# First eight attention units of a fused kernel: diagonal by a second product, natural k through TensorE, and an order written by hand

## The chip, the cores and the metric

The kernel runs on one core of one Trainium2 chip. The metric is the time of the program on the device in microseconds (us), as the median of several runs. Profiles come from one execution each, recorded by the hardware profiler. Engines are named as in the profile: PE (TensorE), with PEld for its weight loads, DVE (VectorE), ACT (ScalarE), POOL (GpSimd) and SP (SyncE, which here only issues transfers).

## The reference

A linear attention with a decaying state (4 batches, 8 heads, 768 tokens, 48 per head) feeds two feed-forward layers (d_model 384, d_ff 2048, 3072 tokens):

```python
for t in range(S):
    kt, vt, rt = (k[:, :, t], v[:, :, t], r[:, :, t])
    cur = np.einsum('bhd,bhe->bhde', u[None] * kt, vt)
    y[:, :, t] = np.einsum('bhd,bhde->bhe', rt, state + cur)
    state = w[None, :, :, None] * state + np.einsum('bhd,bhe->bhde', kt, vt)
...
h = x @ w_in;  g = np.maximum(0.01 * h, h);  x = g @ w_out     # first layer
h = x @ w_in;  g = h * np.cos(h);            out = g @ w_out   # second layer
```

All is float32.

## The kernel before

**Attention.** The 24 units of work are 128 tokens each, two sub-chunks of 64; six units make one batch, and the state goes from unit to unit. A unit loads k transposed (kst, 112x512), r transposed (into ar or rf_), r and k in natural layout (natt, 384 KB) and v. `prep` (L279 to L292) scales kst by inverse powers of the decay (pt[:, 1]) and r by powers (pt[:, 0]), takes the bonus of the diagonal from natt (times ub, times k, summed per head: bon) and scales natural k by the table kn. `piece_a` (L303 to L334) makes 16 score products pa and 16 state products pu, fills ar with a diagonal matrix of bon by eight ACT activations (L321), lays the scores over it under a mask (copy_predicated, L322), and brings the state forward on DVE (L329 to L333). `piece_y1` makes py, copies it to yo on ACT (L371) and writes it to the memory tensor xt by two transfers on POOL's queue (L374). The first eight units (u < ONE) use this form, with tiles lent from weight buffers that are not yet filled.

**Round trip.** `load_xu` (L436 to L441) reads a unit back from xt into xl, on POOL's queue too. Since its first index is a register (the slow path of the kernel writes another half), the read covers all of xt for the dependence tracker: the write of a unit waits until the read of the unit before has landed. `split_xu` casts to xh on ACT (L445) and takes the residual xl on DVE (L446).

**Feed-forward.** Tokens go in six blocks of 512, d_ff in 16 steps of 128. Every float32 product is three products of reduced precision (xl with wh, xh with wl, xh with wh): ph (L458) for the first matrix, po (L498 to L500) for the second. The weights of a step, w0 to w15, are loaded raw in two copies, wr and wo (768 KB each, two buffers of both, L248 and L251), and decoded by `split_w`: sign of wr on ACT (L266), a mask on DVE (L267), relu into wo on ACT (L269), the product for wh on DVE (L270), three more steps on DVE (L271, L273, L275). A buffer is loaded again when its decode is done.

**Order.** The first entries are a list, `first` (prep, attention, output, load and decode of given units), and only ACT follows it word for word (`manual_schedule`); the other engines' order is the scheduler's, which also places instructions of later steps in between. After the list come three more pieces, then blocks 0 and 1 interleaved: (0,0) to (0,7), (0,8), (1,0), (0,9), (1,1) and so on, with the other pieces of units 5 to 7 due between steps. SP issues loads in program order. One head branch (`tc.If(slow > 0)`, L189) separates what stands before it from what stands behind.

Of the kernel before, what the change touches and what calls it, by code (L numbers as in the profile page):

```python
# [58 lines left out]
def moe_rwkv_kernel(ctx: ExitStack, tc, wT, wq, uu, rs, ks, nat, wmoe, out):  # L59
# [114 lines left out]
    kn = ap_.tile([128, H, D], F32, name="kn")
    ps = psum.tile([128, H, D], F32, tag="a0", name="ps_t")
    for i in range(H):
        for c in range(2):
            nc.tensor.matmul(
                out=ps[TOK[c], i], lhsT=(pw[HALF[0], i] if c else pt[HALF[1], 1, i]),
                rhs=ident[ROWS[c], ROWS[c]], start=True, stop=True)  # L180
    nc.scalar.copy(out=kn, in_=ps)
# [96 lines left out]

    def prep(u):  # L279
        t, x, ar = U["nat", u], U["ks", u], ar_[u % 2]  # L280
        bon = ap_.tile([128, H], F32, tag="bon", bufs=2, name="bon")
# [1 line left out]
        if u < ONE:
            nc.vector.tensor_tensor(out=rf_[u % 4], in0=rf_[u % 4], in1=pt[:, 0], op=ALU.mult)
        else:
            for c in range(2):
                nc.vector.tensor_tensor(out=ar[ROWS[c], c], in0=ar[ROWS[c], c], in1=pt[ROWS[c], 0], op=ALU.mult)
# [353 lines left out]
```

## Time and profile before

| what | us |
|---|---|
| median of 3 runs (959.82 to 960.3) | 959.87 |
| span of the profiled execution | 954.9 |
| first MoE product (block 0) | 78.41 |
| first MoE product of block 1 | 137.57 |

Busy in the span: PE 896.4 us (94%), DVE 647.5 (68%), ACT 521.7 (55%), POOL 53.1 (6%). The busy tenths of PE in 40 slices are 1, 6, 4, 8 and then 9 nearly to the end. A busy PE need not be at its peak; the granted clock and the duration of equal products tell its level. A row of the timeline gives start, duration, engine, line, operation, output<-inputs, shapes and count, and in brackets how long the engine had been idle and what released it.

### The profile page before, as it was taken

Reading aid. Unit: us, or ns where it says so; the run is one execution under the profiler, and the core shown is the slowest. Engines: PE = TensorE matmul, PEld = TensorE weight load, DVE = VectorE, ACT = ScalarE, POOL = GpSimd, SP = SyncE. Lnnn points to the kernel's source line nnn. Section 1 sums busy time; section 2 is a strip of 40 time slices with the busy share of each in tenths; the row PEclk is TensorE's granted clock in tenths of the full one; section 3 lists DMA queues with packets and bytes.
Section 4 is the critical chain, followed back from the end, with each engine's and each line's share of the span. In section 5 each row is a group of like instructions: output and inputs, shape, how many; then the busy total and the mean of one; then the engine's idle time right before and its main releaser. Section 6 shows DMA issues by size and latency. Waiting matters only on the chain.

```text
span 954.9 us, 15397 instructions
## 1 busy us (share of the span) xinstructions
PE 896.4 (94%) x5954; PEld 734.8 (77%) x5954; DVE 647.5 (68%) x1072; ACT 521.7 (55%) x1050; POOL 53.1 (6%) x92
## 2 busy tenths in 40 slices
PE   1648979999999999999999999999999999999997
PEld 1646858887778888878888788888888888888886
DVE  7768979449865776675848877565665755665654
ACT  1435545635654564563645566665665655665654
POOL 3111100000100000001000000000000000000000
PEclk9957989999999999999999999999999999999999
DMA  7579786024512322252828910100100100100000
GB/s 191 160 248 310 257 287 187 1 68 131 174 47 65 114 98 89 95 204 74 306 69 276 314 72 1 33 34 1 34 34 1 62 4 9 59 1 0 34 1 34
DMA packets 41277, 99.79 MB, mean 104 GB/s; under 512 B 4976, under 2 KB 8176, under 8 KB 41200
## 3 DMA queue, kind: packets, MB, share of 16 engines
q1 hardware_dynamic: 31552, 75.96, 24.6%
q0 software_dynamic: 4896, 14.16, 4.7%
q10 hardware_dynamic: 4752, 8.65, 2.4%
q8 instruction: 47, 0.77, 0.3%
q14 instruction: 30, 0.25, 0.1%
HBM read 84.59 MB, written 14.16 MB: 103 GB/s over the span
## 4 chain that ended last, share of the span: by engine, by line
PE 75%; DMA 10%; DVE 8%; ACT 3%; issue 2%; SPq 0%; POOL 0%; POOLq 0%; ACTq 0%; DVEq 0%
PE ph L458 35%; PE po L498 12%; PE po L499 12%; PE po L500 12%; DMA wr<-in_wmoe 2%; DMA xl<-xt 2%; PE pa L309 2%; PE py L346 2%; ACT ar L321 1%; DMA natt<-in_nat 1%; DMA xt<-yo 1%; PE pu L316 1%; DVE wh L270 1%; DVE wl L275 1%; DMA wo<-in_wmoe 1%
## 5 line engine op out<-in xcount | busy, mean ns | idle before, releaser
L498 PE MATMUL po<-gh,wl 128*128 128x512 f32 x576 | 228.0, 396 | 2.9 <-ACT gh L485 2.7
L499 PE MATMUL po<-gh,wh 128*128 128x512 f32 x576 | 224.6, 390 | 0.0
L500 PE MATMUL po<-gl,wh 128*128 128x512 f32 x576 | 207.0, 391 | 0.7 <-DVE gl L486 0.7
L486 DVE TENSOR_TENSOR gl<-ga,gh 128x512 fp32r<-128x512 f32 x192 | 132.2, 689 | 94.7 <-ACT gh L485 80.6
L485 ACT CAST gh<-ga 128x512 fp32r<-128x512 f32 x192 | 118.6, 619 | 120.1 <-PE po L499 73.3
L458 PE MATMUL ph<-xl,wh 128*128 128x512 f32 x576 | 169.1, 396 | 5.9 <-DVE xl L446 4.8
L458 PE MATMUL ph<-xh,wh 128*128 128x512 f32 x576 | 168.1, 391 | 0.0
L458 PE MATMUL ph<-xh,wl 128*128 128x512 f32 x576 | 165.0, 392 | 0.0
L458 PEld LDWEIGHTS ph<-xl,wh 128*128 128x128 f32 x576 | 108.2, 190 | 30.7 <-DVE xl L446 5.2
L498 PEld LDWEIGHTS po<-gh,wl 128*128 128x128 f32 x576 | 108.1, 188 | 28.0 <-ACT gh L485 4.1
L458 PEld LDWEIGHTS ph<-xh,wl 128*128 128x128 f32 x576 | 109.0, 189 | 23.1
L500 PEld LDWEIGHTS po<-gl,wh 128*128 128x128 f32 x576 | 107.9, 188 | 24.4 <-DVE gl L486 1.8
L458 PEld LDWEIGHTS ph<-xh,wh 128*128 128x128 f32 x576 | 109.0, 189 | 23.0
L499 PEld LDWEIGHTS po<-gh,wh 128*128 128x128 f32 x576 | 108.2, 188 | 21.4
L321 ACT ACTIVATE ar<-ident,bon 64x64 f32<-64x64 f32 (+1 forms) x320 | 80.7, 333 | 26.6 <-DVE bon L290 26.3
L473 DVE SCALAR_TENSOR_TENSOR gt<-gt,ga 128x512 f32<-128x512 f32 x96 | 65.8, 689 | 38.9 <-ACT gt L472 38.4
L468 DVE TENSOR_TENSOR ga<-ph,ga 128x512 f32<-128x512 f32 x96 | 66.0, 688 | 37.8 <-ACT ga L467 37.4
L478 DVE TENSOR_TENSOR ga<-ph,gt 128x512 f32<-128x512 f32 x96 | 65.8, 689 | 36.3 <-ACT gt L477 35.7
L467 ACT ACTIVATE ga<-ph 128x512 f32<-128x512 f32 x96 | 57.1, 594 | 59.2 <-PE ph L458 56.1
L477 ACT ACTIVATE gt<-gt 128x512 f32<-128x512 f32 x96 | 59.8, 627 | 49.8 <-DVE gt L475 49.7
L471 ACT ACTIVATE ga<-ph 128x512 f32<-128x512 f32 x96 | 57.4, 598 | 44.3 <-PE ph L458 30.3
L472 ACT ACTIVATE gt<-ga 128x512 f32<-128x512 f32 x96 | 60.2, 631 | 1.6
(128 smaller groups left out, 754.0 us busy)
## 6 DMA issues: line engine op xcount, KB each, us to landing
wr<-in_wmoe SPq DMA_DIRECT2D x32, 768.0 KB, 6.0
wo<-in_wmoe SPq DMA_DIRECT2D x32, 767.5 KB, 5.7
natt<-in_nat SPq DMA_DIRECT2D x20, 384.0 KB, 4.1
xt<-yo POOLq DMA_DIRECT2D x48, 96.0 KB, 3.6
x2t<-ob ACTq DMA_DIRECT2D x18, 256.0 KB, 2.0
xl<-x2t POOLq DMA_DIRECT2D x6, 768.0 KB, 4.7
kst<-in_ks SPq DMA_DIRECT2D x20, 224.0 KB, 3.4
vs<-in_nat SPq DMA_DIRECT2D x40, 96.0 KB, 4.1
```

The lines of the kernel that those rows point to most:

```text
L321: nc.scalar.activation(out=ar[q, c, g], in_=ident2[q], func=AF.Copy, scale=bon[q, g:g + 1])
L458: nc.tensor.matmul(out=p, lhsT=w_[:, 0, k * 128:(k + 1) * 128], rhs=x_[:, k], start=(m == 0), stop=(m == 3 * KT - 1))
L468: nc.vector.tensor_tensor(out=ga, in0=p, in1=ga, op=ALU.max)
L472: nc.scalar.activation(out=gt, in_=ga, func=AF.Copy, bias=MAGIC)
L473: nc.vector.scalar_tensor_tensor(out=gt, in0=gt, scalar=MAGIC, in1=ga, op0=ALU.subtract, op1=ALU.subtract)
L477: nc.scalar.activation(out=gt, in_=gt, func=AF.Sin, scale=-TWOPI)
L478: nc.vector.tensor_tensor(out=ga, in0=p, in1=gt, op=ALU.mult)
L485: nc.scalar.copy(out=gh, in_=ga)
L486: nc.vector.tensor_tensor(out=gl, in0=ga, in1=gh.bitcast(F32), op=ALU.subtract)
L498: nc.tensor.matmul(out=o, lhsT=w_l[:, 1, sl], rhs=gh, start=(f == 0), stop=False)
L499: nc.tensor.matmul(out=o, lhsT=w_h[:, 1, sl], rhs=gh, start=False, stop=False)
L500: nc.tensor.matmul(out=o, lhsT=w_h[:, 1, sl], rhs=gl, start=False, stop=(f == NF - 1))
```

## The change

For units 0 to 7 the natural copies of r and k are no longer loaded. Z is scaled k times u and w per head (uw, from a small transposed copy uT). The diagonal comes from a second set of 16 products pd = Z with r, laid in by a second copy_predicated with ident2 as mask. Natural k comes from 16 products pk of kst with an identity or with dg, a diagonal of decay powers, and an ACT copy. For units 0 to 3 the old state enters the accumulation by products with the identity and dg, and ACT copies write the states; units 4 to 7 ("lean") bring the state forward on DVE as before. Every second unit's output uses a second yo tile. The clears of tiles on POOL stand behind dg. The list `first` has finer steps, and ACT, DVE and PE follow it; kn is computed behind it. Loads of units 1 to 3 are issued ahead of the branch.

```diff
@@ load
-        nc.sync.dma_start(out=n, in_=src[:, 0:2])
+        if u >= ONE:
+            nc.sync.dma_start(out=n, in_=src[:, 0:2])
...
     load(0)
+    nc.sync.dma_start(out=ut, in_=uT)
+    for u in range(1, 4):
+        load(u)
...
+    nc.vector.tensor_tensor(out=uw, in0=ut, in1=ws, op=ALU.mult)
...
+    nc.gpsimd.memset(dg, 0.0)
     nc.gpsimd.tensor_tensor(
-        out=pw[HALF[0]], in0=pt[HALF[0], 1], in1=late.to_broadcast([D, H, HC]), op=ALU.mult)
...
+        out=dg[HALF[0]], in0=ident[HALF[0], HALF[0]].unsqueeze(1).to_broadcast([D, H, D]),
+        in1=late.to_broadcast([D, H, D]), op=ALU.mult)
...
+    def flip(src):
+        return [(c, g, src[ROWS[c], g], dg[HALF[0], g] if c else ident[HALF[1], HALF[1]])
+                for g in range(H) for c in range(2)]
+    def early(u):
+        x, r, z, ar, vs = kf_[u % 4], rf_[u % 4], zf_[u % 2], ar_[u % 2], v_of(u)
+        n, st = nk_[u % 2], ss_[u % 3]
...
+        first, lean = u % NCH == 0, u >= UB
...
+            tag = {"pk": "a1", "pa": "a0", "pd": "a2", "pu": "a1"}[k] if lean else \
+                {"pk": "o1", "pa": ("a0", "o2")[u % 2], "pd": "h", "pu": ("a1", "o0")[u % 2]}[k]
...
+        def Z():
+            nc.vector.tensor_tensor(
+                out=z, in0=x, in1=uw.unsqueeze(2).to_broadcast([PACK, H, HC]), op=ALU.mult)
+        def PK():
+            o = bank_of("pk")
+            for c, g, a, b in flip(x):
+                nc.tensor.matmul(out=o[TOK[c], g], lhsT=a, rhs=b, start=True, stop=True)
+        def NK():
+            nc.scalar.copy(out=n, in_=p.pop("pk"))
...
+        def PU():
+            o = bank_of("pu")
+            fold = not first and not lean
+            if fold:
+                nc.tensor.matmul(out=o[HALF[1]], lhsT=ident[0:PACK, HALF[1]], rhs=st[0:PACK, 0], start=True, stop=False)
...
+        def S1():
+            if not lean:
+                nc.scalar.copy(out=s1, in_=p["pu"][HALF[1]])
...
+        def PV():
+            if not last and not lean:
+                for g in range(H):
+                    nc.tensor.matmul(
+                        out=p["pu"][HALF[0], g], lhsT=dg[:, g], rhs=st[0:PACK, 1, g], start=False, stop=g == H - 1)
...
-        yo = ap_.tile([PACK, H, HC], F32, tag="yo", bufs=YOB, name="yo")
+        yo = yo1 if u % 2 else ap_.tile([PACK, H, HC], F32, tag="yo", bufs=YOB, name="yo")
...
-    first = [("p", 0), ("a", 0), ("p", 1), ("a", 1), ("y", 0), ("p", 2), ("a", 2), ("y", 1), ("d", 0),
-             ("p", 3), ("a", 3), ("y", 2), ("l", 4), ("d", 1), ("y", 3), ("l", 5), ("d", 2), ("p", 4)]
+    first = [("X R Z PK PA PD NK", 0), ("X R Z", 1), ("PU S1 PV M N S0", 0), ("PK PA PD NK", 1), ("X R Z", 2),
+             ("y", 0), ("PU S1 PV M N S0", 1), ("PK PA PD NK", 2), ("d", 0), ("X R Z", 3), ("y", 1),
+             ("PU S1 PV M N S0", 2), ("PK PA PD NK", 3), ("d", 1), ("x", 0), ("y", 2), ("l", 4),
+             ("PU S1 PV M N S0", 3), ("x", 1), ("y", 3), ("l", 5), ("d", 2), ("x", 2), ("X R Z", 4)]
...
-    with tc.manual_schedule(engines={mybir.EngineType.Activation}):
+    with tc.manual_schedule(engines={mybir.EngineType.Activation, mybir.EngineType.DVE, mybir.EngineType.PE}):
```

How instructions stand on an engine before and after is shown at three places. First ACT, from the copy of unit 1's output (yo) to that of unit 3's, in the kernel before. A wr row with one operand is the sign of a weight step, a wo row its relu; 362 is w0 and 366 is w1:

```order
L371 COPY yo_596<-py_563 112x512
L445 CAST xh_507<-xl_508 128x3x128
L266 ACTIVATE wr_362<-wr_362 128x768
L269 ACTIVATE wo_364<-wr_362,rebias_343 128x768
L321 ACTIVATE ar1_75<-ident2_133,bon_616 128x64 x8
L371 COPY yo_702<-py_669 112x512
L445 CAST xh_507<-xl_508 128x3x128
L266 ACTIVATE wr_366<-wr_366 128x768
L269 ACTIVATE wo_368<-wr_366,rebias_343 128x768
L371 COPY yo_760<-py_727 112x512
```

The same in the changed kernel, from behind unit 1's copy on; 352 is the relu of w1, 756 and 886 are the raw copies of w3 and w4, and unit 2's copy is yo_795, unit 3's lent_wl12_88:

```order
L274 ACTIVATE wo_352<-wr_350,rebias_342 128x768
L550 CAST xh_527<-xl_528 128x3x128
L271 ACTIVATE wr_756<-wr_756 128x768
L274 ACTIVATE wo_758<-wr_756,rebias_342 128x768
L476 COPY yo_795<-py_762 112x512
L350 COPY lent_wh15_78<-pu_804 48x384
L679 COPY kn_897<-ps_t_898 128x384
L271 ACTIVATE wr_886<-wr_886 128x768
L367 COPY lent_wl15_79<-pu_804 48x384
L550 CAST xh_527<-xl_528 128x3x128
L274 ACTIVATE wo_888<-wr_886,rebias_342 128x768
L476 COPY lent_wl12_88<-py_836 112x512
```

Ahead of unit 2's copy there were the steps of w0 and now there are those of w1 and w3; ahead of unit 3's there were those of w1 and now also w4's; the activations of L321 are gone.

The second place is ACT around the copy of unit 4's output, yo_889 in the kernel before, where 723 is w3, 612 w2 and 781 w4:

```order
L266 ACTIVATE wr_723<-wr_723 128x768
L445 CAST xh_507<-xl_508 128x3x128
L266 ACTIVATE wr_612<-wr_612 128x768
L269 ACTIVATE wo_725<-wr_723,rebias_343 128x768
L269 ACTIVATE wo_614<-wr_612,rebias_343 128x768
L371 COPY yo_889<-py_856 112x512
L266 ACTIVATE wr_781<-wr_781 128x768
L445 CAST xh_507<-xl_508 128x3x128
```

In the changed kernel the copy is yo_1034; 1372 is w7, 1517 w8 and 1597 w9, and ga and gh are the first MoE step:

```order
L550 CAST xh_527<-xl_528 128x3x128
L271 ACTIVATE wr_1372<-wr_1372 128x768
L274 ACTIVATE wo_1374<-wr_1372,rebias_342 128x768
L271 ACTIVATE wr_1517<-wr_1517 128x768
L572 ACTIVATE ga_1053<-ph_1043 128x512
L274 ACTIVATE wo_1519<-wr_1517,rebias_342 128x768
L590 CAST gh_1069<-ga_1053 128x512
L271 ACTIVATE wr_1597<-wr_1597 128x768
L476 COPY yo_1034<-py_1001 112x512
```

The copy stood ahead of the last cast of block 0 and of w4's sign; now it stands behind that cast, behind w7 and w8 and behind w9's sign.

The third place is PE where MoE products begin, in the kernel before with unit 5's scores and state products ahead and unit 4's py further up:

```order
L367 MATMUL py_856<-ar0_74,lent_wl15_79 48x64 x2
L316 MATMUL pu_945<-vs1_77,natt_88 48x48 x8
L458 MATMUL ph_898<-xl_508,wh0_603 128x512 x3
L458 MATMUL ph_898<-xh_507,wl0_604 128x512 x3
L458 MATMUL ph_898<-xh_507,wh0_603 128x512 x3
```

In the changed kernel, with unit 4's scores (pa), diagonal (pd) and state products (pu):

```order
L326 MATMUL pa_942<-ar0_74,kst_83 64x64 x16
L326 MATMUL pd_959<-ar0_74,natt_89 64x64 x16
L339 MATMUL pu_976<-vs0_76,lent_wh12_87 48x48 x8
L344 MATMUL pu_976<-vs0_76,lent_wh12_87 48x48 x8
L563 MATMUL ph_1043<-xl_528,wh0_612 128x512 x3
L563 MATMUL ph_1043<-xh_527,wl0_613 128x512 x2
L468 MATMUL py_1001<-ar0_74,vs0_76 64x64
L468 MATMUL py_1001<-ar0_74,vs0_76 48x64
L472 MATMUL py_1001<-ar0_74,lent_wl15_79 48x64
```

Unit 4's py, which stood ahead of the first MoE product, now stands behind five of them. Counted over the whole list, 162 MoE products stood ahead of the first one of block 1, and now 157 do.

## Rows read from the trace of the kernel before

**Rows 1.** Stretches: us, busy us (instructions) per engine, PEclk, DMA share, GB/s
```profile
0.00:12.00 12.00, 0.61 (x4) 0.37 (x4) 8.76 (x24) 1.89 (x2) 8.51 (x26) 1.00 0.43 116
12.00:34.00 22.00, 11.33 (x196) 10.45 (x197) 16.14 (x29) 5.72 (x21) 0.74 (x2) 1.00 0.92 281
...
56.00:78.40 22.40, 10.99 (x176) 10.01 (x176) 17.95 (x31) 11.00 (x25) 4.67 (x6) 0.50 0.66 208
78.40:100.00 21.60, 21.60 (x191) 16.87 (x191) 19.52 (x34) 13.57 (x33) 2.11 (x3) 0.89 0.93 316
...
120.00:137.60 17.60, 10.94 (x46) 7.73 (x44) 12.56 (x21) 7.92 (x12) 2.03 (x3) 0.91 0.93 297
137.60:160.00 22.40, 22.40 (x91) 18.40 (x92) 19.92 (x32) 12.50 (x18) 0.00 (x0) 0.92 0.80 258
```

**Rows 2.** Timeline of PE: first product of block 0, then block 1
```profile
78.41 1.65 PE L458 MATMUL ph<-xl,wh 128*128 128x512 f32 x3
...
137.57 1.65 PE L458 MATMUL ph<-xl,wh 128*128 128x512 f32 x3 [4.76 <-DVE xl L446]
...
143.55 0.84 PE L458 MATMUL ph<-xl,wh 128*128 128x512 f32 x3
144.23 0.84 PE L458 MATMUL ph<-xh,wl 128*128 128x512 f32 x3
```

**Rows 3.** Timeline of PE: score products of three units, end of unit 0's py
```profile
27.54 1.97 PE L309 MATMUL pa<-ar,kst 48*64 48x64 f32 x32 [2.31 <-DVE ar L322]
...
32.43 0.28 PE L367 MATMUL py<-ar,lent_wh 112*48 112x64 f32 x2
...
71.64 1.97 PE L309 MATMUL pa<-ar,kst 48*64 48x64 f32 x31
...
94.41 1.15 PE L309 MATMUL pa<-lent_wh,lent_wh 48*64 48x64 f32 x32
```

**Rows 4.** Timeline of POOL: table product, then writes of units 0 to 4 and 7
```profile
11.31 1.13 POOL L172 TENSOR_TENSOR pw<-pt,wc 48x512 f32<-48x512 f32 x1 [2.18 <-DVE pt L170]
33.70 1.47 POOL L374 DMA_DIRECT2D xt<-yo  x2 [21.26 <-ACT ar L321]
...
42.09 1.60 POOL L374 DMA_DIRECT2D xt<-yo  x2 [3.34 <-ACT xh L445]
...
51.10 1.27 POOL L374 DMA_DIRECT2D xt<-yo  x2 [4.31 <-ACT xh L445]
...
63.97 1.27 POOL L374 DMA_DIRECT2D xt<-yo  x2 [4.29 <-ACT wr L266]
...
76.57 1.64 POOL L374 DMA_DIRECT2D xt<-yo  x2 [4.07 <-ACT wr L266]
...
123.10 1.27 POOL L374 DMA_DIRECT2D xt<-yo  x2 [6.72 <-ACT xh L445]
```

**Rows 5.** SP's issue of w2's wo; then issues from 30 to 60 us
```profile
47.66 0.37 SPq L251 DMA_DIRECT2D wo<-in_wmoe  x1
...
wo<-in_wmoe SPq DMA_DIRECT2D x1, 767.5 KB, 5.1
```

**Rows 6.** Timeline of ACT: activations of unit 0, sign and relu of w1
```profile
23.29 2.02 ACT L321 ACTIVATE ar<-ident,bon 128x64 f32<-128x64 f32 x8 [8.35 <-DVE bon L290]
...
50.98 0.93 ACT L266 ACTIVATE wr<-wr 128x768 f32<-128x768 f32 x1
56.18 1.00 ACT L269 ACTIVATE wo<-wr,rebias 128x768 int32<-128x768 int32 x1 [4.27 <-DVE wr L267]
```

**Rows 7.** Timeline of DVE: reciprocals; products for wh of w0, w1, w3
```profile
7.77 3.37 DVE L170 RECIPROCAL pt<-pw 112x256 f32<-112x256 f32 x2
...
44.50 0.96 DVE L270 TENSOR_TENSOR wh<-wo,wr 128x768 fp32r<-128x768 f32 x1 [1.03 <-ACT wo L269]
...
57.53 0.95 DVE L270 TENSOR_TENSOR wh<-wo,wr 128x768 fp32r<-128x768 f32 x1
...
69.92 0.96 DVE L270 TENSOR_TENSOR wh<-wo,wr 128x768 fp32r<-128x768 f32 x1
```

More of the change, by code (lines that the diff above doesn't have):

```diff
@@ L171, in moe_rwkv_kernel @@
     nc.gpsimd.tensor_tensor(out=wc, in0=wc, in1=wc, op=ALU.mult)
+    dg = ap_.tile([PACK, H, D], F32, name="dg")
+    nc.gpsimd.memset(dg, 0.0)
     nc.gpsimd.tensor_tensor(
-        out=pw[HALF[0]], in0=pt[HALF[0], 1], in1=late.to_broadcast([D, H, HC]), op=ALU.mult)
[L174 to L181, printed above, removed]
+        out=dg[HALF[0]], in0=ident[HALF[0], HALF[0]].unsqueeze(1).to_broadcast([D, H, D]),
+        in1=late.to_broadcast([D, H, D]), op=ALU.mult)
+    for t in ar_:
+        nc.gpsimd.memset(t[:, 0], 0.0)
+    for t in vf_:
+        nc.gpsimd.memset(t[64:128, 0], 0.0)
+        nc.gpsimd.memset(t[0:64, 1], 0.0)
+    for t in ss_:
+        nc.gpsimd.memset(t, 0.0)
     ub = ap_.tile([128, H, D], F32, name="ub")
-    nc.sync.dma_start(out=ub, in_=uu)
     sm = ap_.tile([D, H, D], F32, name="sm")
@@ L279, in prep, with step @@
+    E = {}
+    def step(names, u):
+        e = E.setdefault(u, early(u))
+        for k in names.split():
+            e[k]()
     def prep(u):
+        if u < ONE:
+            return step("X R Z", u)
         t, x, ar = U["nat", u], U["ks", u], ar_[u % 2]
@@ L282, in prep @@
         nc.vector.tensor_tensor(out=x, in0=x, in1=pt[:, 1], op=ALU.mult)
[L283 to L287, printed above, removed]
+        for c in range(2):
+            nc.vector.tensor_tensor(out=ar[ROWS[c], c], in0=ar[ROWS[c], c], in1=pt[ROWS[c], 0], op=ALU.mult)
         nc.vector.tensor_tensor(out=t[:, 0], in0=t[:, 0], in1=ub, op=ALU.mult)
@@ L303, in piece_a @@
     def piece_a(u):
+        if u < ONE:
+            return step("PK NK PA PD PU S1 PV S0 M N", u)
         x, bon, ar, vs = U.pop(("ks", u)), U.pop(("bon", u)), ar_[u % 2], v_of(u)
@@ L565, in moe_rwkv_kernel @@
                 load_xu(u)
-                if u:
-                    split_xu(u - 1)
+    nc.sync.dma_start(out=ub, in_=uu)
+    kn = ap_.tile([128, H, D], F32, name="kn")
+    ps = psum.tile([128, H, D], F32, tag="a1", name="ps_t")
+    for c, g, a, b in flip(pt[:, 1]):
+        nc.tensor.matmul(out=ps[TOK[c], g], lhsT=a, rhs=b, start=True, stop=True)
+    nc.scalar.copy(out=kn, in_=ps)
     load(6)
@@ L616 @@
     wq = np.ascontiguousarray(np.stack([w, u], 0))
+    uT = np.ones((PACK, H), np.float32)
+    uT[0:D] = uT[64:PACK] = u.T
     uu = np.ascontiguousarray(np.broadcast_to(u.reshape(1, H, D), (C, H, D)))
```

83 lines of the change are left out of this document (65 added, 18 removed).

## The prediction

> **What bounds the kernel now.** I read the busy table by stretch first. From the first product of block 1 on, TensorE never stands: 22.40 us busy of 22.40 from 137.6 us [rows 1], and the rest of the page looks the same. Before it there is slack: TensorE is busy about half of 12 to 34 and of 56 to 78.4 us, all of 78.4 to 100, and 10.94 of the last 17.60 [rows 1]. So the total is the start of block 1 (137.57 us, after 4.76 us of waiting for the last residual [rows 2]), plus a constant, plus whatever matrix products remain to be done then. That start, T1, is what I forecast. In steady flow three products take 144.23 - 143.55 = 0.68 us [rows 2], 0.227 each.
>
> Second I read what T1 hangs on, the round trips over memory. Unit 0's result is issued to memory at 33.70, unit 1's at 42.09, unit 2's at 51.10, unit 3's at 63.97, unit 4's at 76.57, unit 7's at 123.10 [rows 4]. The read back of a unit touches the whole of xt, so the next write waits for its landing, on POOL's queue: one trip is at least 8.4 us (33.70 to 42.09), and 12.6 when weights load beside it (63.97 to 76.57) [rows 4]. The first MoE product starts at 78.41 [rows 2], when unit 3 has come back. From unit 7's write to block 1 it takes 137.57 - 123.10 = 14.5.
>
> Third, the weights. Raw copies exist twice. Between two decodes in one buffer lie: product for wh at 44.50 to the reissue of wo at 47.66, 3.2 us; load 5.1; the ACT step that needs it, 1.0 [rows 5 to 7]. That is a floor of 9.3 us; the kernel before takes 69.92 - 57.53 = 12.4 for one [rows 7]. In ACT's queue the decode steps stand before copies of results, so a late load delays a round trip: the step at 56.18 had stood 4.27 us for its mask, which itself waited on loads [rows 6].
>
> **The change, part by part.**
>
> *Loads.* Eight natural loads of 384 KB go, 3.07 MB. At the 281 GB/s of 12 to 34 us [rows 1] that is 10.9 us of transfer, of which the four early ones (5.5 us) lie in that busy stretch and the others beside weights. The weight loads themselves wait for buffers, so I count this within the floor below, not beside it. The weights' first issue moves earlier too, which hides: their first use is at the decode of w0.
>
> *Head.* Before, the chain is reciprocal, POOL table, transposes, kn, bonus, eight activations (2.02 us [rows 6]), py. After it: reciprocals end at 7.77 + 3.37 = 11.1 [rows 7], k product 0.7, natural-k products from 11.8, provided that POOL has dg by then: one clear and one product of 48x384, against the 48x512 product that starts at 11.31 after 2.18 us of idle and takes 1.13 [rows 4]. The clears of v and state tiles (13 of them) now stand behind dg; at 8.51 us for 26 instructions [rows 1] they take 4.3 us and are done by about 17, before pu wants them. Sixteen products of 64 columns take 1.97 us here and 1.15 at the higher clock [rows 3]; of 48 columns I take three quarters, 1.5. In the low state: pk 1.5, the branch 1.2 (estimate), pa 2.0, pd 2.0, to 18.5. Then, in the high state, pu 0.9, state copy 0.6, fold 0.5, pk 0.9, pa 1.15, pd 1.15 of unit 1, py half of 32.71 - 29.44 (the pa before it starts at 27.54 and takes 1.97 [rows 3]), 1.65: 25.4, and 1.0 from py's end to the write as now (32.71 to 33.70 [rows 3, 4]). Unit 0 is written at 26.4 instead of 33.70, 7.3 us earlier.
>
> *Clock.* The granted clock reads 0.50 in 56 to 78.4 and the same sixteen score products take 1.97 there (71.64) as at 27.54; at 94.41, in a stretch that reads 0.89, 1.15 [rows 1, 3]. So 27.54 was at 1.2 GHz too, after 2.31 us of idle (the reading of 1.00 there [rows 1] I set aside), and 94.41 at 2.4 GHz. Whether products with an identity lift the clock as others do no row decides: the only ones of before stood among idle time. I take that they do. The Trainium skill ("TensorE: Matmul & The Clock Gate", Part 4: PE-mode transpose) says that the clock does not engage for transpose-mode products, as they do not count as busy in the same way; no run here shows that, and the added products are ordinary ones against an identity. By that rule the head would be rival C.
>
> *Second product for the diagonal.* Per unit it takes away eight ACT activations (2.02) and adds Z and a second selection, about 0.7 us each on DVE, against three bonus steps and the kn product that go; on TensorE 1.15 (pd) and 0.9 (pk) more. In the head the difference is in the sum above; for units 4 to 7 it lies on a full TensorE (below).
>
> *Order, first stretch.* This is where I expect the gain to go. The order lists show ACT's queue: ahead of unit 2's copy stand both steps of w1 and both of w3; ahead of unit 3's copy also w4; ahead of the third cast w2. Before, unit 2's copy stood behind w0 only and unit 3's behind w1. w0 is decoded at about 32 and w1 at 40 (before: 44.50, 57.53). w1, w3, w4, w5, w7 and w9 share one buffer. At the floor their decodes come at 40, 49, 58.5, 68, 77, 86.5; at 12.4 each at 40, 52, 65, 77, 90, 102. I take 10.5, nearer the floor since DVE has less to do: 40, 49, 60, 72, 82, 92.5. Unit 2's copy then comes at 48.4 (write 48.7, before 51.10) and unit 3's at 59.6 (write 60, before 63.97); reading it back and the last cast, behind the activation step of w6, gives the first MoE product at about 76.5, 1.9 earlier. Of 7.3 us, 5.4 are gone, to decodes that have been put in front.
>
> *Order, second stretch.* Unit 4's copy, which before preceded the decode of the weights after w4, now stands behind the sign of w9; that needs w7's buffer (82), a load of 5.1 and 0.93: 88. TensorE's order has changed too: unit 4's py stands behind five products of the first MoE step, which costs 2 us and is hidden. Write of unit 4 at 88.6, before 76.57: 12 us late. Three trips to unit 7 at 8.4 to 12.6, I take 11, the mean with loads beside some: 121.6; 14.5 from there to block 1: 136; 2 us for unit 5's copy behind w11. T1 = 138. With ends: 88.6 + 25.2 + 14.5 = 128 and 88.6 + 37.8 + 14.5 = 141.
>
> *TensorE as the bound of that stretch.* Before, 78.41 to 137.57 is 59.2 us, minus 6.7 of standing (17.60 - 10.94): 52.5, of which 162 products at 0.227 are 36.8 and the rest 15.7 is attention and slow start. After: by the order lists 157 products precede block 1: 35.6; 15.7; and 3 × 2.05 of pd and pk for units 5 to 7: 57.5. From 76.5 that is 134, so TensorE can't start block 1 earlier, and the chain says 138. A new wait: pd of the next unit takes the bank of py, so it waits for the copy of the unit before; behind it on TensorE stand MoE products. I take it within the 4 us between the two.
>
> **Sum**, against the profiled execution: span 954.9, about 5 us around it, beside the median 959.87. T1 moves 138 - 137.57 = +0.4; five products that come after T1 instead of before it, 5 × 0.227 = +1.1. 959.87 + 1.5 = **961.4**.
>
> **Rivals.**
> A, the forecast: the head's gain is eaten by decodes in front of copies. Range by the ends of T1, TensorE's 134 and the chain's 141: 957.4 to 964.4; with 1.5 either way for the estimates (branch, cycle of 10.5), 956 to 966.
>
> B, faster: the buffers run at the 9.3 floor, since 3.07 MB less traffic and fewer DVE steps (some 8 x 0.8 us) remove the waits. Then the copies of units 3 and 4 come with the data and not behind decodes, the first MoE product at 72, unit 4's write near 80, and TensorE is the bound: 72 + 57.5 = 129.5, total 959.87 - 8.1 + 1.1 = 952.9, range 950 to 957. For it: DMA is only 0.66 busy from 56 to 78 [rows 1]. Against it: waits in front of copies were already there before with fewer decodes in front [rows 6].
>
> C, slower: the identity products don't raise the clock, so the head stays at 1.2 GHz: the 6.85 us of TensorE work after 18.5 that I took in the high state (pu to py without the copy) take about 5 us more. Every decode, copy and trip shifts by it, T1 143, total 966.4; from 964 to 970. It decides if the score products of unit 1 take near 1.97. For it: the score products at 27.54 were still at that level [rows 3]; against it, they came after waits, and the new head has fewer.
>
> **How the numbers follow.** Chances: A 0.44, B 0.34, C 0.22. What a measurement of this kernel can tell from no change is about 0.2%, 1.9 us: 957.95 to 961.79. Of A I put 0.06 below, 0.24 within, 0.14 above. Faster 0.34 + 0.06 = 0.40; same 0.24; slower 0.14 + 0.22 = 0.36. The likeliest alone has 956 to 966. For 8 in 10 I go from 951.5, which leaves out the lower part of B, to 968.5, which leaves out the end of C.
>
> **What would show it.** Unit 0's write near 26 and unit 1's scores at 1.15 us (head; 1.97 is C). Copies of units 2 and 3 at 48 and 60, with decode steps waiting for loads just ahead of them on ACT. First MoE product at 76 to 77. Unit 4's copy near 88 behind a sign that waited for a load; if it comes at 80, B is right. Block 1 at 138. I am wrong at the root if anything after block 1 differs, for instance if TensorE stands there, or if the natural loads were on the path of weights (then decodes come closer than 9.3 apart).

## The result, and the profile after it

The changed kernel takes 971.5 us (median of 4 runs, 969.12 to 973.03) against 959.85 for the kernel before (4 runs, 958.14 to 960.3): ratio 1.0119, 95% interval 1.0097 to 1.0141, so some 11.6 us slower. The forecast was 961.4 with a range of 951.5 to 968.5; the time lies above its end. The profiled run of the changed kernel took 969.12, its span is 967.5 against 954.9.

First the stretches of the changed kernel, in the columns of [rows 1]:

```profile
12.00:34.00 22.00, 20.81 (x493) 19.77 (x491) 8.45 (x14) 5.73 (x10) 2.23 (x3) 1.00 0.54 178
...
56.00:78.40 22.40, 7.09 (x149) 6.97 (x146) 16.96 (x28) 8.83 (x12) 3.03 (x4) 0.58 1.00 309
...
120.00:137.60 17.60, 17.60 (x280) 15.20 (x280) 12.03 (x19) 5.71 (x11) 3.03 (x5) 1.00 0.22 69
...
160.00:200.00 40.00, 39.43 (x173) 31.85 (x172) 21.07 (x35) 20.17 (x53) 0.00 (x0) 1.00 0.03 8
200.00:900.00 700.00, 697.83 (x4308) 571.63 (x4307) 467.89 (x768) 399.06 (x800) 26.11 (x42) 1.00 0.26 84
```

The head is fuller: TensorE is busy 20.81 of 22 us, not 11.33. From 56 to 78.4 us it is emptier than before (7.09 against 10.99), with the transfers at 1.00. From 120 to 137.6 it is full (17.60 against 10.94), with 280 instructions instead of 46: small attention products. From 160 us on TensorE is full, as before.

The timeline of TensorE of the changed kernel, the rows that answer to [rows 2] and [rows 3]:

```profile
21.93 1.11 PE L326 MATMUL pa<-ar,kst 48*64 48x64 f32 x32
...
81.64 0.96 PE L563 MATMUL ph<-xl,wh 128*128 128x512 f32 x3 [0.44 <-DVE xl L551]
93.16 1.15 PE L326 MATMUL pd<-ar,natt 48*64 48x64 f32 x32 [2.51 <-ACT yo L476]
94.24 1.27 PE L339 MATMUL pu<-vs,lent_wh 128*48 128x48 f32 x16
110.06 1.97 PE L326 MATMUL pd<-lent_wh,natt 48*64 48x64 f32 x32 [3.00 <-ACT lent_wl L476]
...
150.14 0.85 PE L563 MATMUL ph<-xl,wh 128*128 128x512 f32 x3
```

The first product of block 0 starts at 81.64 (before 78.41), that of block 1 at 150.14 (before 137.57): 12.57 us later, which is the 12.6 us of the span. Twice pd stands, for a copy of yo. Block 1 itself is not kept waiting: its product has no waiting time in the row, where [rows 2] had 4.76 us, and the last residual of its tokens (timeline of DVE) was done 1.3 us before:

```profile
148.25 0.55 DVE L551 TENSOR_TENSOR xl<-xl,xh 128x384 fp32r<-128x384 f32 x1
```

The timeline of POOL in the changed kernel, the writes of units 0 to 7 and, at 60.43, the read back of unit 2 ([rows 4] before):

```profile
26.91 1.47 POOL L479 DMA_DIRECT2D xt<-yo  x2 [15.30 <-ACT yo L476]
35.22 1.28 POOL L479 DMA_DIRECT2D xt<-lent_wl  x2 [3.49 <-ACT lent_wl L476]
53.81 1.27 POOL L479 DMA_DIRECT2D xt<-yo  x2 [12.69 <-ACT yo L476]
60.43 0.75 POOL L546 DMA_DIRECT2D xl<-xt  x1 [5.35 <-DMA xt<-yo]
68.29 1.27 POOL L479 DMA_DIRECT2D xt<-lent_wl  x2 [7.11 <-DMA xl<-xt]
93.40 1.27 POOL L479 DMA_DIRECT2D xt<-yo  x2 [17.68 <-ACT yo L476]
...
110.30 1.27 POOL L479 DMA_DIRECT2D xt<-lent_wl  x2 [8.39 <-ACT lent_wl L476]
...
126.03 1.41 POOL L479 DMA_DIRECT2D xt<-yo  x2 [9.26 <-ACT yo L476]
...
136.73 1.27 POOL L479 DMA_DIRECT2D xt<-lent_wl  x2 [4.03 <-ACT lent_wl L476]
```

Units 0 and 1 are written 6.8 and 6.9 us earlier than before. Unit 2 is 2.7 us late, unit 3 4.3, unit 4 16.8, unit 7 13.6. Unit 3's write waited for the read back of unit 2 to land, not for its own copy.

The timeline of ACT in the changed kernel shows what stands in front of the copies of units 2, 3 and 5 ([rows 6] before):

```profile
48.42 0.90 ACT L271 ACTIVATE wr<-wr 128x768 f32<-128x768 f32 x1 [6.24 <-DMA wr<-in_wmoe]
...
52.04 1.01 ACT L274 ACTIVATE wo<-wr,rebias 128x768 int32<-128x768 int32 x1 [2.72 <-DMA wo<-in_wmoe]
52.93 0.58 ACT L476 COPY yo<-py 112x512 f32<-112x512 f32 x1
...
59.90 0.88 ACT L271 ACTIVATE wr<-wr 128x768 f32<-128x768 f32 x1 [5.38 <-DMA wr<-in_wmoe]
...
62.89 0.58 ACT L476 COPY lent_wl<-py 112x512 f32<-112x512 f32 x1
...
108.49 1.05 ACT L274 ACTIVATE wo<-wr,rebias 128x768 int32<-128x768 int32 x1 [2.43 <-DMA wo<-in_wmoe]
109.42 0.59 ACT L476 COPY lent_wl<-py 112x512 f32<-112x512 f32 x1
```

Each copy stands behind decode steps that waited for a load (6.24 and 2.72 us, 5.38, 2.43). Unit 3's copy was done near 63.5, 4.8 us ahead of its write, so there the decodes cost nothing; the delay came with unit 2's late write and its read back. For unit 5's copy, the chain of work that ended last in the changed kernel passes through weight loads, here two loads of wo with a decode in between, up to the step at 108.49:

```profile
94.13 7.59 DMA wo<-in_wmoe
...
103.20 5.21 DMA wo<-in_wmoe
```

Last, what TensorE did between the first product of block 0 and the first of block 1, by tile. Columns: stretch, busy of PE (instructions), clock, DMA share, GB/s. In the kernel before, first all engines as above, then ph, po, pa, pu and py:

```profile
78.41:137.57 59.16, 52.50 (x468) 41.03 (x467) 51.33 (x85) 32.18 (x60) 7.45 (x10) 0.93 0.88 294
78.41:137.57 59.16, 22.69 (x82) 0.93 0.88 294
78.41:137.57 59.16, 21.28 (x81) 0.93 0.88 294
78.41:137.57 59.16, 2.61 (x64) 0.93 0.88 294
78.41:137.57 59.16, 1.94 (x65) 0.93 0.88 294
78.41:137.57 59.16, 7.31 (x176) 0.93 0.88 294
```

In the changed kernel all engines, then ph, po, pa, pd, pk, pu and py:

```profile
81.64:150.14 68.50, 62.13 (x765) 52.41 (x766) 50.16 (x79) 29.36 (x44) 8.24 (x12) 0.93 0.58 194
81.64:150.14 68.50, 21.67 (x81) 0.93 0.58 194
81.64:150.14 68.50, 19.22 (x76) 0.93 0.58 194
81.64:150.14 68.50, 3.34 (x96) 0.93 0.58 194
81.64:150.14 68.50, 4.22 (x96) 0.93 0.58 194
81.64:150.14 68.50, 3.40 (x96) 0.93 0.58 194
81.64:150.14 68.50, 5.28 (x80) 0.93 0.58 194
81.64:150.14 68.50, 8.48 (x240) 0.93 0.58 194
```

The stretch grew by 9.34 us. Feed-forward products (ph, po) went from 43.97 to 40.89, attention from 11.86 to 24.72, standing from 6.66 to 6.37: -3.1, +12.9, -0.3 (products overlap a little, by 3.3 and 3.5 us). Of the 12.9, pk and pd are 7.6, pu grew by 3.3, and py and pa by 1.9. Unit 4's py and unit 5's scores and state products used to stand ahead of the stretch.

### The profile page after: what moved, and what is told of

It reads as the page before. It is cut to its first block, busy times and chain, and to the rows that moved or that the text cites. A ratio compares the mean times of both kernels' runs of the same rounds, so it can differ in the third digit from the quotient of the medians.

```text
span 967.5 us, 16493 instructions
## 1 busy us (share of the span) xinstructions
PE 915.4 (95%) x6536; PEld 755.5 (78%) x6536; DVE 636.8 (66%) x1045; ACT 514.4 (53%) x1002; POOL 53.0 (5%) x95
## 4 chain that ended last, share of the span: by engine, by line
PE 76%; DMA 9%; DVE 9%; ACT 2%; issue 2%; POOL 1%; SPq 0%; POOLq 0%; ACTq 0%; DVEq 0%
PE ph L563 34%; PE po L603 12%; PE po L604 11%; PE po L605 11%; DMA wo<-in_wmoe 5%; DMA wr<-in_wmoe 2%; PE py L451 1%; PE pa L415 1%; DVE wh L275 1%; DVE wl L280 1%; DVE ga L573 1%; PE pu L422 1%; DMA lent_wl<-in_ks 1%; DVE wr L272 1%; DVE gl L591 1%
## 5 line engine op out<-in xcount | busy, mean ns | idle before, releaser
L604 PEld LDWEIGHTS po<-gh,wh 128*128 128x128 f32 x576 | 108.4, 188 | 21.4
L427 ACT ACTIVATE ar<-ident,bon 64x64 f32<-64x64 f32 x256 | 64.5, 333 | 16.7 <-DVE bon L394 16.4
```

The lines of the kernel that those rows point to most:

```text
L427: nc.scalar.activation(out=ar[q, c, g], in_=ident2[q], func=AF.Copy, scale=bon[q, g:g + 1])
L604: nc.tensor.matmul(out=o, lhsT=w_h[:, 1, sl], rhs=gh, start=False, stop=False)
```

## The experiments

My theory after the result: the head's gain goes first to ACT's order (forecast A), then to a TensorE that has more attention between 78 and 160 us. The rival: the operations are harmless, and only the places in which steps were put cost the time. All kernels compute everything unless a text says otherwise. For each, the table has the median, the ratio to the kernel before on the same chip, and in the stretch 78 to 160 us of its profile TensorE's standing (82 us less its busy time) and the attention products, summed by tile. (Some expectations have lower figures for attention, 11.0, 26.5 and 19.4 for the kernel before, the changed one and e6; they are not these sums.) The medians come from several chips, so two kernels are best compared by their ratios. Executions of one kernel differ by several us, those of g3 from 965.13 to 971.35, and each profile is one execution.

| kernel | median us | ratio [95%] | standing | attention |
|---|---|---|---|---|
| before | 959.85 | | 6.7 | 12.3 |
| changed | 971.5 | 1.0119 [1.0097, 1.0141] | 7.1 | 28.0 |
| e1_w3_behind | 970.3 | 1.0105 [1.0066, 1.0144] | 9.4 | 32.7 |
| e2_act_by_hand | 970.1 | 1.0106 [1.0060, 1.0153] | 9.6 | 27.5 |
| e3_coarse_list | 970.14 | 1.0111 [1.0063, 1.0158] | 13.0 | 21.4 |
| e5_x4_early | 970.55 | 1.0122 [1.0076, 1.0168] | 9.1 | 26.5 |
| e6_e1_x4_early | 965.94 | 1.0066 [1.0050, 1.0083] | 11.6 | 20.8 |
| e7_old_4_to_7 | 975.75 | 1.0185 [1.0140, 1.0230] | 12.4 | 18.5 |
| e8_e1_old_4_to_7 | 983.98 | 1.0284 [1.0239, 1.0329] | 29.3 | 16.7 |
| f5_unit4_by_hand | 970.73 | 1.0119 [1.0085, 1.0153] | 13.8 | 20.2 |
| f4_hand_old_5_to_7 | 974.07 | 1.0140 [1.0074, 1.0206] | 20.7 | 11.6 |
| g1_pu_in_halves | 973.69 | 1.0151 [1.0108, 1.0193] | 10.7 | 25.1 |
| g3_e6_pu_in_halves | 968.73 | 1.0085 [1.0059, 1.0111] | 11.6 | 19.8 |
| g2_pd_twice | 977.71 | 1.0176 [1.0141, 1.0211] | 9.6 | 36.5 |
| f1_before_more_pe | 986.02 | 1.0278 [1.0208, 1.0348] | 21.9 | 20.1 |
| h1_yo_on_dve | 978.62 | 1.0193 [1.0160, 1.0225] | 11.2 | 32.7 |
| h5_yo_dve_pu_halves | 979.87 | 1.0219 [1.0184, 1.0255] | 12.4 | 26.5 |
| h4_g3_yo_on_dve | 966.65 | 1.0082 [1.0054, 1.0110] | 9.6 | 19.9 |
| h2_h4_nk_on_dve | 972.29 | 1.0153 [1.0124, 1.0182] | 19.0 | 19.5 |

None is faster than the kernel before.

### Is it the order of the first stretch?

e1 names the decode of w3 in the list, behind unit 3's copy:

```diff
-             ("PU S1 PV M N S0", 3), ("x", 1), ("y", 3), ("l", 5), ("d", 2), ("x", 2), ("X R Z", 4)]
+             ("PU S1 PV M N S0", 3), ("x", 1), ("y", 3), ("l", 5), ("d", 2), ("d", 3), ("x", 2), ("X R Z", 4)]
```

> The changed kernel, with the decode of w3 put into the hand list behind that of w2, so that the copies of units 2 and 3 no longer stand behind decode steps of w3 and w4 on ACT. Theory O (copies behind decodes make the round trips late): unit 2 is written near 45 instead of 53.8, unit 3 near 56 instead of 68.3, the first MoE product comes at 68 to 72 instead of 81.6, and the total falls by at least half of that, to 960 to 966. Theory L (the trips are long because weights and unit loads are in the queues beside them, whatever ACT does): the copies move but the landings don't, total 969 or more. Theory W (more work on TensorE in the stretch of blocks 0 and 1): 971, whatever comes earlier.

It did free the copies: units 2 and 3 are written at 48.52 and 62.12, not 53.81 and 68.29, and the first product of block 0 comes 8.3 us earlier. The total didn't move. Its timelines of TensorE and of POOL, the write of unit 4:

```profile
73.31 1.65 PE L563 MATMUL ph<-xl,wh 128*128 128x512 f32 x3 [19.88 <-DVE xl L551]
...
100.97 1.27 POOL L479 DMA_DIRECT2D xt<-yo  x2 [34.31 <-ACT yo L476]
```

Unit 4 is written at 100.97, later still than 93.40. (This execution took 976.42, the longest of e1's five, and its unit 0 is written only at 31.50.) So the decodes in front of the copies of units 2 and 3 are real and alone do not set the total: what they cost is lost again further on.

e3 takes the list of before with the new operations (only ACT by hand), e2 keeps e1's list and puts ACT in hand order through the second stretch too (with AHEAD = 3).

```diff
-    first = [("X R Z PK PA PD NK", 0), ("X R Z", 1), ("PU S1 PV M N S0", 0), ...
-    with tc.manual_schedule(engines={mybir.EngineType.Activation, mybir.EngineType.DVE, mybir.EngineType.PE}):
+    first = [("p", 0), ("a", 0), ("p", 1), ("a", 1), ("y", 0), ("p", 2), ("a", 2), ("y", 1), ("d", 0), ...
+    with tc.manual_schedule(engines={mybir.EngineType.Activation}):
```

> The changed kernel with the list of the kernel before: whole steps (scale, attention, output, decode, load) in the old order, and only ACT held to it. Loads, second products, natural k and states in the accumulation stay. Theory O: what costs time is the order and not the new operations, so unit 2's copy stands behind w0 only, unit 3's behind w1; first MoE product near 70, total 958 to 964. Theory W: the operations cost it, 968 to 974.

> As e1_w3_behind, and ACT follows the program's order up to the last attention piece of units 4 to 7, with each weight decoded two steps ahead of its use; units 4 to 7 are then copied behind w3, w5, w7 and w10 or so, instead of behind w9, w11 and later ones. Theory O: unit 4 is written near 75 instead of 93.4, block 1 starts at 130 to 140, total 952 to 962. Theory L: total within 4 us of e1_w3_behind. Theory W: block 1 can't start before the first MoE product + 60, so a total more than 8 us below e1 speaks against it.

Both come out at the changed kernel's time, although their first products of block 0 lie 15 us apart (e3 at 75.6, e2 at 90.9), and e2 writes unit 4 at 90.12 and not near 75. Neither the finer list nor the scheduler's order of ACT is the whole cause. A last one issues the loads of units 6 and 7 between later steps, which changes what these units compute:

```diff
-    load(6)
-    load(7)
...
+            if slot == (0, 3):
+                load(6)
+                load(7)
```

> The changed kernel with the loads of units 6 and 7 issued some 10 us later, behind the weights of the next step; as a side effect the scheduler also puts unit 4's copy behind w5 instead of w9. Theory L: the read back of unit 2, 7.9 us from issue to landing (60.4 to 68.3), falls to 5 to 6, unit 3 is written near 66, total 966 to 969. Theory O: units 2 and 3 stay where they are to within 2 us and the first MoE product at 80 to 82, but unit 4's write comes near 85 and the total falls to 962 to 967.

It took 976.55 (1.0183 [1.0144, 1.0222]); nothing is concluded from it.

### Unit 4's place

Two rows of DVE of the changed kernel, the residual of unit 2 and the scaling of unit 4's k (X of unit 4):

```profile
72.18 0.55 DVE L551 TENSOR_TENSOR xl<-xl,xh 128x384 fp32r<-128x384 f32 x1
72.65 0.68 DVE L305 TENSOR_TENSOR kst<-kst,pt 112x512 f32<-112x512 f32 x1
```

and the same scaling in the kernel before:

```profile
54.98 0.69 DVE L282 TENSOR_TENSOR kst<-kst,pt 112x512 f32<-112x512 f32 x1 [1.64 <-DMA kst<-in_ks]
```

In the hand list ("X R Z", 4) stands behind ("x", 2), which waits for unit 2's round trip; DVE follows the list, so unit 4 starts 17.7 us later and its attention falls into the full stretch. e1 has it at 73.17, still behind that residual. e5 moves it forward; e6 does that and e1's edit:

```diff
-             ("PU S1 PV M N S0", 3), ("x", 1), ("y", 3), ("l", 5), ("d", 2), ("x", 2), ("X R Z", 4)]
+             ("PU S1 PV M N S0", 3), ("x", 1), ("X R Z", 4), ("y", 3), ("l", 5), ("d", 2), ("d", 3), ("x", 2)]
```

> The changed kernel with one entry of the hand list moved: the scaling of unit 4 (X R Z) stands ahead of unit 3's output instead of behind the residual of unit 2, which waits for a read back. Theory X (unit 4 starts late because DVE's list holds its scaling behind that residual): unit 4's scaled k at 55 to 60 instead of 72.7, its write near 80 instead of 93.4, block 1 at 138 to 142 instead of 150, total 960 to 965. Theory C (each of units 4 to 7 has a longer chain: natural k goes over TensorE, ACT and TensorE again, each time behind decodes and MoE products, and its second product waits for the copy of the unit before): unit 4 comes earlier but the next writes fall back, total 968 or more.

> e1_w3_behind with the same entry moved. Theory X: first MoE product at 73, unit 4's write at 76 to 80 instead of 101, block 1 near 135, total 953 to 960. Theory C: total 965 or more although both earlier stretches are ahead of the kernel before.

e5 alone changes nothing. Its scaling of unit 4 comes at 66.17, not at 55 to 60 as expected, because the residual ahead of it waits for a cast that stands on ACT behind a weight's sign, which had waited 4.90 us for its load; unit 4 is written at 89.84. e6 gives about 5 us of the 11.6 back: 5.6 by the medians, 5.1 by the ratios (the two intervals don't meet). Its four executions lie within 1 us; g3 below, with the same order on ACT and DVE, reaches only 1.0085, 3.3 us below the changed kernel, with intervals that overlap. The timelines of DVE and of POOL in e6, and its stretch from 78 to 160:

```profile
58.62 0.68 DVE L305 TENSOR_TENSOR kst<-kst,pt 112x512 f32<-112x512 f32 x1
...
78.59 1.27 POOL L479 DMA_DIRECT2D xt<-yo  x2 [14.18 <-ACT yo L476]
...
78.00:160.00 82.00, 70.42 (x716) 57.30 (x715) 66.86 (x108) 37.15 (x56) 8.62 (x12) 0.94 0.75 247
```

Unit 4 is scaled at 58.62 (a scaling at 55.80, after 8.64 us of waiting for a load, is unit 5's, which the scheduler put ahead of it) and written at 78.59, near the 76.57 of [rows 4]. Its products leave the stretch (attention 20.8 instead of 28.0), and part of that turns into standing (11.6 instead of 7.1). Block 1 starts at 144.82, 5.3 us earlier than in the changed kernel. The profiles of e1 and e5 write unit 0 at 31.5 and that of e6 at 27.41, so some of the distance between them can be that of their heads (last section). f5 goes further and puts all of unit 4 into the list:

```diff
+             ("PK PA PD NK PU S1 PV M N S0", 4), ("d", 2), ("x", 2), ("y", 4), ("d", 3), ("x", 3)]
```

> e6_e1_x4_early with all of unit 4 (products, copies, output, last cast) in the hand list ahead of the first MoE product. Theory W: unit 4's products go back into the stretch in which TensorE stands, attention behind the first MoE product falls below e6's 19.4 us by about the rest of unit 4, total 960 to 965, still above the kernel before by units 5 to 7's 3 x 2.9 us. Theory O: below 958.

It loses e6's gain again: unit 4 is written at 75.99, but the first product of block 0 comes at 87.54, after 3.62 us of waiting for unit 3's residual, which the list puts behind unit 4's output.

### The old form for units 4 to 7

e7 keeps the changed kernel's list and gives units 4 to 7 the old operations (natural loads, bonus, activations); e8 adds e1's edit; f4 is f5 with units 5 to 7 in the old form.

```diff
-        if u >= ONE:
+        if u >= UB:
             nc.sync.dma_start(out=n, in_=src[:, 0:2])
...
-        if u < ONE:
+        if u < UB:
             return step("PK NK PA PD PU S1 PV S0 M N", u)
```

> The changed kernel with units 4 to 7 in the old form: natural r and k loaded (4 x 384 KB), bonus and natural k on DVE, eight activations, one score product, and one yo tile; units 0 to 3 as changed; unit 4's scaling is left to the scheduler. Theory C: with the shorter chain the writes of units 4 to 7 come at the spacing of the kernel before, block 1 at 134 to 140, total 957 to 963. Theory X: no better than e5_x4_early by more than 2 us.

> e1_w3_behind with units 4 to 7 in the old form. Theory C: first MoE product near 73, block 1 at 130 to 135, total 952 to 958, the best so far. Theory X: as e6_e1_x4_early within 2 us.

> As f5_unit4_by_hand, but units 5 to 7 in the old form (natural loads, bonus on DVE, eight activations, one score product). Theory W: attention behind the first MoE product falls to the 9 to 12 us of the kernel before; with the first product at 73 instead of 78 the total is 952 to 958, below the kernel before and 7 to 9 below f5. Theory O: within 2 us of f5.

None is faster than the changed kernel: e8 is clearly slower, e7 by 4 us with intervals that just meet, f4 by less than its interval. In e7 the granted clock of the stretch is lower too (0.82 against 0.92). The stretch from 78 to 160 of f4:

```profile
78.00:160.00 82.00, 61.26 (x519) 49.09 (x520) 70.75 (x116) 45.56 (x82) 9.15 (x12) 0.90 0.85 280
```

Attention is at 11.6 us, below the kernel before, and TensorE stands 20.7. So taking the new products away isn't enough: with the old ones, standing takes their place. That speaks against a theory of TensorE's load alone, and for a second cause: the placement of steps, or the loads, since the old form also brings the natural loads back (DMA share 0.85 here, 0.65 in the changed kernel). These runs don't separate the two.

### One operation at a time, with the order kept

g1 makes the state products of units 4 to 7 over 64 tokens each, as the old form did, and leaves nearly all rows of the other engines in their places. g3 does the same to e6, where the order of ACT, DVE, SP and POOL is unchanged.

```diff
+            if lean:
+                for g in range(H):
+                    for c in range(1 if last else 2):
+                        nc.tensor.matmul(
+                            out=o[ROWS[c], g], lhsT=n[TOK[c], g], rhs=vs[TOK[c], c, g], start=True, stop=True)
+                return
```

> The changed kernel with the state products of units 4 to 7 made as before, over the 64 tokens of a sub-chunk, two of them side by side in the array, instead of over all 128 rows of which half are zeros. The order on every engine stays as in the changed kernel but for a few rows. Theory W (TensorE's time on attention between 78 and 160 us sets the end): pu takes 1.1 to 1.2 us less in three and a half units, total 2 to 5 us below the changed kernel. Theory S (the places of waiting copies and decodes set it, TensorE's time is hidden): within 1.5 us of it.

> e6_e1_x4_early with the state products of units 4 to 7 over halves; the order of ACT, DVE, SP and POOL is exactly that of e6. Theory W: total 2 to 4 us below e6, 962 to 964. Theory S: 965 to 967.

Two lines of g1's stretch, pu alone and then all, and a row of its TensorE:

```profile
78.00:160.00 82.00, 4.63 (x112) 0.93 0.65 210
78.00:160.00 82.00, 71.25 (x851) 59.12 (x848) 60.84 (x95) 35.53 (x54) 8.30 (x12) 0.93 0.65 210
...
96.19 1.47 PE L326 MATMUL pd<-ar,natt 48*64 48x64 f32 x32 [3.40 <-ACT yo L482]
```

pu fell from 7.69 to 4.63 in 78 to 160, and standing rose from 7.1 to 10.7. No gain in either pair. In g1, unit 4's copy of yo comes at 95.56 instead of 92.54, again behind decode steps that waited for loads, and unit 5's pd waits 3.40 us for it instead of 2.51; unit 6's pd no longer waits 3.00 us, but other waits stand in its place (2.14 for unit 3's residual, 1.29 for natural k, 2.06 for a state). So a shorter TensorE was worth nothing here, while the waits moved.

g2 makes pd of units 4 to 7 twice; f1 makes the score products of units 4 to 7 three times in the kernel before:

```diff
-            for g in range(H):
+            for g in list(range(H)) * (2 if lean and k == "pd" else 1):
...
+        for _ in range(3 if UB <= u < ONE else 1):
```

> The changed kernel with pd of units 4 to 7 made twice (the same values again), 16 products more a unit, 1.1 us at the higher clock and 2.0 at the lower; order nearly the same. Theory W: total 4 to 7 us above the changed kernel. Theory S: within 1.5 us.

> The kernel before, with the 16 score products of units 4 to 7 made three times (the same values again), which adds to TensorE about what the changed kernel's pk and pd add: 2.3 us a unit at the higher clock, and nothing else. Theory W (time of attention on TensorE behind the first MoE product is what counts: it went from 11.0 us to 26.5 us between 78 and 160 us, and MoE products lost as much): units 5 to 7 lie there, so 3 x 2.3 = 6.9 us less MoE, total 4 to 8 us above the kernel before. Theory O (only the place of copies and decodes counts): the 6.7 us that TensorE stands before block 1 hide it, total within 2 us.

g2 has 6.1 us more of pd (11.19 against 5.09) and its median is 6.2 us above the changed kernel's (5.5 by the ratios; the intervals just touch). Its profile writes unit 0 at 31.40, so part of its figures can be the head's. f1 adds some 9 us of products and is 26 us slower; its steps were placed anew by the scheduler, and it stands 21.9 us. So added products cost about their length in g2, as far as its head allows to say, and much more in f1, and f1 says that an edit's own cost can't be read where the order moves with it.

### The copy on another engine

h1 moves the yo copies of units 4 to 7 to DVE; h5 adds g1's halves to that; h4 is g3 with these copies on DVE; h2 is h4 with the natural copy NK there too.

```diff
-        nc.scalar.copy(out=yo, in_=py)
+        (nc.vector.tensor_copy if u >= UB else nc.scalar.copy)(out=yo, in_=py)
...
-            nc.scalar.copy(out=n, in_=p.pop("pk"))
+            (nc.vector.tensor_copy if lean else nc.scalar.copy)(out=n, in_=p.pop("pk"))
```

> The changed kernel with the copies of units 4 to 7's outputs on DVE instead of ACT, so that they no longer stand behind the sign and activation of a weight that is still loading; some 60 of 5100 rows of the order change. Theory S (unit 4's copy behind w9's sign, unit 5's behind w11's step): unit 4's write moves from 93.4 to 89 or 90, pd of unit 5 and 6 no longer wait 2.5 and 3.0 us for a copy, total 2 to 5 us below the changed kernel. Theory W (TensorE's time): within 1.5 us.

> h1_yo_on_dve and g1_pu_in_halves together, at nearly the same order. If both limits lie close to each other (the time that g1 took from TensorE came back as standing before pd, which waits for a copy), the two together give what neither gives alone: total 4 to 8 us below the changed kernel, 963 to 967. If neither is the limit: 970 to 973.

> g3_e6_pu_in_halves with the copies of units 4 to 7 on DVE. Theory S: total 2 to 5 us below e6 and g3, 961 to 964. Theory W: as g3, 964 to 969.

> h4_g3_yo_on_dve with the copies of natural k of units 4 to 7 on DVE too. If the longer chain (TensorE, ACT behind decodes, TensorE) still delays units 5 to 7: 2 to 4 us below h4. If not: within 1.5 us of it.

On the changed kernel's order it is 7 us worse. A row of DVE of h1:

```profile
90.78 0.56 DVE L276 TENSOR_SCALAR wo<-wo 128x768 int32<-128x768 int32 x1 [1.78 <-DMA wo<-in_wmoe]
```

DVE too has decode steps that wait for loads, and unit 4's copy comes at 98.43 there instead of 92.54; 4.4 us of that lag h1 has already at unit 3's write (72.71), from a late head. With the halves besides (h5) it is no better, and there the head is early: unit 3 is written at 68.42, as in the changed kernel, and unit 4 at 98.98. On g3's order it is neither better nor worse (1.0082 against 1.0085), and with NK on DVE too (h2) it loses: standing rises from 9.6 to 19.0.

## Why the prediction was wrong, step by step

**Right: what bounds the kernel.** The total is the start of block 1 plus a constant: +12.57 at block 1, +12.6 in the span, and a full TensorE behind 160 us. The extra 1.1 us for five products that now come after block 1's start does not show beside these. The forecast's "about 5 us around" the span is no overhead: the changed kernel's executions take 1.6 to 1.7 us more than their spans, so the profiled execution of the kernel before was probably some 3 us shorter than its median. The sum doesn't use it.

**Right in this run: the head.** Unit 0 is written at 26.91 (forecast 26.4) and unit 1's scores take 1.11 us, the level of 2.4 GHz, so rival C didn't hold in the profiled run. The 1.2 us that the sum takes for the branch come from no row; the first scores follow the first natural-k products without a gap (13.20, while these run from 11.08 to 13.6). The clears on POOL stood ahead of dg's product (2.49 to 9.7, then 10.33) and not behind it, and rival C's 6.85 us is 6.25 without the copy; neither matters to the result. A late head does occur (last section), and isn't what decided: the profiled execution of h4 writes unit 0 at 30.46 and takes 966.51, that of g3 at 26.77 and takes 965.73.

**Right in kind, too small: decodes in front of copies.** Units 2 and 3 are copied at 52.93 and 62.89, where the forecast had 48.4 and 59.6, with waiting decodes just ahead. The trip from unit 2's write to unit 3's took 14.5 us (53.81 to 68.29), of which 7.9 is the read back with DMA at 1.00; the forecast had 48.7 to 60, and 12.6 as its longest trip. The first product of block 0 is 81.64 instead of 76.5: 5.1 us. Two errors partly cancel there: unit 3's write is 8.3 us later than forecast, and the way from it to the first product 3.2 us shorter (13.3 instead of 16.5).

**Wrong: the second stretch.** This is the term that failed. It was sized in two ways, both short.

By trips, the forecast took 88.6 for unit 4's write, 3 × 11 to unit 7, and 14.5 + 2 to block 1. Measured: 93.40, then 43.3 (14.4 each), then 13.4. So 4.8, 10.3 and -3.1. The 11 was chosen between trips of the first stretch, though [rows 4] hold the same leg: 76.57 to 123.10 is 46.5, or 15.5 each. With that the same sum gives 88.6 + 46.5 + 16.5 = 151.6, near the measured 150.14. That it comes so near is in part luck: the three trips were 21.1, 12.4 and 13.1 us before and are 16.9, 15.7 and 10.7 now. In the rows of POOL these three writes had waited 8.39, 9.26 and 4.03 us for ACT's copy and not directly for a read back. What held the copies differs: unit 5's stood behind a step that waited for its weight load (2.43 us), unit 6's waited 1.30 us for TensorE's py, and unit 7's stood behind a cast that had waited 2.72 us for unit 6's read back. And block 1 did not wait for the last trip, as the forecast had it; TensorE reached it 1.3 us after the residual was there.

By TensorE, the forecast took 57.5 us of products and 4 of standing from 76.5. Measured from 81.64: 62.13 and 6.37. The late start gives 5.1, the products 4.6, the standing 2.4, together the 12.1 by which block 1 missed 138. The forecast had 6.7 us too little attention, for three reasons; about 2 came back, mostly because the feed-forward products took 3.1 us less than before and not 1.1. pk and pd of three units took 3.40 + 4.22 = 7.6, not 6.15, one pd at 1.97 after standing. The growth of pu by 3.3 was not costed at all. Of it, 1.3 is unit 5's pu, which moved in (row at 94.24 above; a batch's last unit makes half the products). The rest is the shape: a whole unit over 64 tokens took 0.89 in the kernel before (row of TensorE), and unit 7's over 128 rows takes 1.50 (busy time of pu in a stretch, columns as above; the granted clock is 1.00 in both), unit 6's 2.51 where the granted clock is 0.50, just after pd had stood 3.00 us:

```profile
95.39 0.89 PE L316 MATMUL pu<-lent_wh,lent_wh 64*48 64x48 f32 x32
...
127.50:130.00 2.50, 1.50 (x32) 1.00 0.87 310
```

The Trainium skill ("TensorEngine Tiling (Array Packing)", Theoretical Speedup) gives a dimension of at most 64 a tiling factor of two and up to twice the speed. The trace agrees with "up to": 1.50 to 0.89 us for a unit here is 1.7 times, and all of pu went from 7.69 to 4.63 us in g1. And the move of unit 4's py behind five products was called hidden, and that of unit 5's scores not seen; they bring 1.9 us more of py and pa into a stretch that hides nothing.

**Wrong: the new wait of pd** was placed within 4 us of slack. It is 2.51 and 3.00 in two rows, most of the 6.37 us that TensorE stands before block 1, so there was no slack to hide it in.

**Cause, as far as shown.** Of 11.6 us, 3 to 5 come from two places in the hand list together (w3's decode in front of copies, unit 4's scaling behind a residual), by e6 and g3; either alone gives nothing. The other 6 to 8 stay open: e6 still has 8.5 us more attention and 5 us more standing than the kernel before, e7 and f4 show that old products bring more standing, g1 and g3 that fewer product microseconds bring none back. One rival is untested: the weights, two buffers of each copy, whose loads and decodes stand in the chain of the changed kernel up to 109 us. No run gives them another buffer. What share belongs to the operations and what to the places in which the scheduler fills in decodes could not be separated, since nearly every edit moves those places. Whether an order exists that brings the head's 7 us to the end wasn't found.

## What to carry to other kernels

Before a leg of a chain is given a length, take the length which that same leg has in the trace of before, and not that of a quieter stretch, and ask what ends each wait in it. For each engine, add up what will lie in the bounding stretch, with every product that moves in or takes a larger shape, since there nothing hides it. In an order written by hand, an item that needs a round trip delays all that follows on its engine: put work that needs no more than a load ahead of it.

## What the runs showed of the hardware

The clock of the head differs between kernels whose head has the same order. The row of unit 1's scores in e1:

```profile
23.35 1.94 PE L326 MATMUL pa<-ar,kst 48*64 48x64 f32 x32
```

It reads 1.94 us there, the level of 1.2 GHz, and 1.11 in the changed kernel and in e6, e7, e8, g1, g3, h2 and h5; e1, e2, e5, f4, f5, g2, h1 and h4 have the long one, and write unit 0 at 30.2 to 31.6 instead of 26.4 to 27.4. All these have one profile each, so what sets it is open. The Trainium skill ("TensorE: Matmul & The Clock Gate", Part 4: PE-mode transpose) says that the full clock doesn't engage for transpose-mode products; the ordinary products against an identity here stand in front of both, and the runs don't decide whether they count.
